# Four weight loads and splits moved within the projections of a two-branch attention kernel

## Chip, core and metric

The kernel runs on one NeuronCore of a Trainium2 chip. The metric is the device time of one execution in microseconds. Before the change it is 1011.23 us, the median of 3 runs (1010.02 to 1012.23).

The engines are named as in the profile: PE is TensorE's matrix multiply and PEld its weight load, DVE is VectorE, ACT is ScalarE, POOL is GpSimd. SP (SyncE) issues the DMAs, all of them here, in one queue.

## The reference

Input x has 2048 tokens of 448 features. Two attention layers with 16 heads of 28 features each run on the same x and are mixed by a gate for each token.

```python
x = A_x                                               # [1, 2048, 448]
g = _sigmoid((x * gate_w).sum(-1, keepdims=True))
# A: linear attention with the Hedgehog feature map
q, k, v = split_heads(x @ A_wqkv)
pq, pk = einsum("bhsd,hdf->bhsf", q, w_phi), einsum(..., k, w_phi)
phi_q = concat([softmax(pq), softmax(-pq)]); phi_k likewise
num = phi_q @ (phi_k^T v);  den = phi_q . sum_s(phi_k) + 1e-6
a = (num / den) @ A_wo
# B: softmax attention
q, k, v = split_heads(x @ B_wqkv)
b = (softmax(q k^T * 28 ** -0.5) v) @ B_wo
return g * a + (1 - g) * b
```

## The kernel before

**Numbers in two halves.** Matrices of the projections are kept as a high part in the type fp32r and a low part, which is the rest. A load from HBM therefore goes through a staging tile: a DMA brings the f32 values, ACT copies them to the high part, and DVE (in places POOL) subtracts the high part from the raw values and writes the low part. For x this gives XH and XL, for weights `w[:, 0]` and `w[:, 1]`. A projection of 512 tokens by 128 columns is 11 matmuls: four row blocks, each with high by high, high by low and (three of them) low by high.

**The order of work.** Each of the compute engines runs its instructions in the order in which the Python program gives them; an instruction waits on semaphores for what it reads and for the buffer that it overwrites. The order on SP's queue is chosen at build time by the scheduler of the language, from the dependences, so a load can move among the stores of other units when a dependence is added to it. SP issues in that order, and stands where an issue waits. Eight semaphores serve the DMAs in turn, so that an issue also waits until the DMA eight places before it has landed.

**The stage of the change.** The first 66 us compute queries and keys of branch B, transposed, in units: unit n is 128 of the 896 columns (m) for 512 tokens (t). `first_units` does units 0 to 3 (all of t = 0, m 0 to 3) while the weights' first 512 columns, wB[0], and x arrive. The loop `for n in range(4, NP)` does units 4 to 19:

- Units 4 to 7 take t = 1, units 8 to 11 t = 2, units 12 to 15 t = 3, all with wB[0]. Units 16 to 19 take m = 4 for the four t, with wB[1], the later 384 columns (wB1).
- `proj_qk(n, ev)` runs the 11 matmuls into a PSUM bank; `keep_qk` evacuates it. ACT (line 592) copies the bank to the high part of a tile `ev`, DVE (line 593) subtracts to its low part, and one DMA of 512 KB (line 594) stores both to the tensor `qkd` in DRAM. There are 4 buffers of `ev`.
- `splits(n + 1)` in round n splits what round n + 1 needs: x's tile t at the rounds 0, 4 and 8, and the two halves of wB1 in rounds 12 and 14.
- `fold(wkA_s, "k", g)` multiplies a quarter of the key weights of branch A (wtk, loaded by `load_fold`) by the folding matrix phi_s, which holds w_phi, so that the feature map's linear part costs no matmul of its own later. It is 4 calls of matmul (8 in the trace), an ACT copy (line 412) and a DVE subtraction (line 413).
- `split_part(wvA_s, "wvA", 450, i)` with `take_lows()` splits a half of the value weights of branch A (lines 143 and 144).
- `mx_unit()` in rounds 16 to 19 is a block of branch B's row maximum: four narrow matmuls into four banks (line 287), two ACT Relus (line 291) and two DVE additions with maximum (line 292). Later rounds have more of them.

The PSUM tiles of units and foldings share one ring of 3 banks (`ps_s`; units 4 to 6 use banks put aside in `later`), and the mx blocks have a ring of 4. After unit 19 the loop over tokens begins: `pk` (with wkA_s), `pva` (with wvA_s) and mx blocks.

**What holds a load back.** A DMA without a dependence may be issued as early as its place on the queue allows. The kernel delays some by letting POOL write a few elements into the destination first: the DMA overwrites them and so has to wait for the copy, which waits for what it reads.

```python
hold = raws[("x", 1)][0][:1, 0, :4]                        # in first_units
nc.gpsimd.tensor_copy(phi_s[:1, :, 0], hold)
...
nc.gpsimd.tensor_copy(wts[nm][:1, :, 0], phi_s[:1, :, 0])  # in load_fold, for "k"
```

So phi_s waits for x's tile 1, and wtk waits for phi_s. The load of wB1 (round 10) has no hold; its staging tile is one of three.

Of the kernel before, what the change touches and what calls it, by code (L numbers as in the profile page):

```python
# [36 lines left out]
def f32(ap):  # L37
    return ap.bitcast(F32)
# [3 lines left out]
def gated_mix_kernel(ctx, tc, xT, wqkB, wvB, wvA, wkAT, wqAT, phi, woA, woB,  # L42
# [7 lines left out]
    nc = tc.nc  # L50
# [12 lines left out]
    def ps_s(nm):  # L63
        return ps.tile([P, 512], F32, tag="s", name=nm, bufs=psn[0])

    def ps_pv(nm):
        return ps.tile([P, 512], F32, tag="pv", name=nm, bufs=1)

    def ps_mx(nm):
        return ps.tile([P, 512], F32, tag="mx", name=nm, bufs=psn[1])  # L70
# [22 lines left out]
    XH = front.tile([P, 4, S], F32R, name="XH")  # L93
# [6 lines left out]
    def weights(place, nm):  # L100
        if place == 1:
            return wp.tile([P, 2, 4, 512], F32R, tag="w1", name=nm)
        if place == 2:
            return front.tile([P, 2, 4, D], F32R, tag="w2", name=nm)
        return wp.tile([P, 2, 4, 450], F32R, tag="w3", name=nm)
# [21 lines left out]
            nc.tensor.matmul(dst[:, :n], l, r, start=i == 0, stop=i == len(todo) - 1,  # L127
                             skip_group_check=True)

    def stage(shape_b, n, src, nm):  # L130
        raw = stg.tile([P, 2, 512], F32, tag="stg", name=nm)
        nc.sync.dma_start(raw[:, :shape_b, :n], src)
        return raw[:, :shape_b, :n]

# [2 lines left out]
    def take_lows():  # L137
        while lows:
            lows.pop(0)()

    def split_weight(w, raw, bs, cs, low=nc.vector, high=nc.scalar.copy):

        high(w[:, 0, bs, cs], raw)
        lows.append(lambda: low.tensor_sub(w[:, 1, bs, cs], raw, f32(w[:, 0, bs, cs])))

    def load_part(src, n, nm, b, parts=2):
        return stage(parts, n, src[:, b:b + parts, :], f"{nm}_raw{b}")

    def weight_part(w, src, n, nm, b, parts=2, low=nc.vector):
        split_weight(w, load_part(src, n, nm, b, parts), slice(b, b + parts), slice(0, n), low)  # L150
# [14 lines left out]
    def take_acts():  # L165
        while acts:
            acts.pop(0)()
# [57 lines left out]
    def pair_query(gq, hp):  # L225
        g, qb = divmod(gq, NQ)
        mxs[("qp", gq, hp)] = mx_rows(mx_tile("qc", f"qp{gq}_{hp}", 3), range(4), q_d[g],
                                      (2 * hp, 2 * hp + 1) * 2, qb * 512)
# [130 lines left out]
    phi_s = bk.tile([112, NG, 112], F32, name="phi_s")  # L359
# [5 lines left out]
    def load_last(b):  # L365

        raw = bd.tile([P, H, 2, DH], F32, tag="feat", name=f"xraw3_{b}", bufs=4)
        raw = raw.rearrange("p h s f -> p (h s f)")[:, :512]
        nc.sync.dma_start(raw, xT[:, b, 1536:])
        return raw  # L370
# [25 lines left out]
    def load_fold(src, nm):  # L396
        wts[nm] = bk.tile([112, NG, 512], F32, tag="wt", name=f"wt{nm}", bufs=1)
        if nm == "k":
            nc.gpsimd.tensor_copy(wts[nm][:1, :, 0], phi_s[:1, :, 0])
        for k in range(NG):  # L400
            nc.sync.dma_start(wts[nm][:, k, :], src[:, k, :])

    def fold(dst, nm, g, b0=0, n=4):

        wt = wts[nm][:, g, :]
        pw = ps_s(f"pw{nm}{g}_{b0}")
        for b in range(n):
            nc.tensor.matmul(pw[:, b * 112:(b + 1) * 112], wt[:, (b0 + b) * P:(b0 + b + 1) * P],
                             phi_s[:, g, :], start=True, stop=True)
        pw3 = pw[:, :n * 112].rearrange("p (b f) -> p b f", f=112)  # L410
        bs, gs = slice(b0, b0 + n), slice(g * 112, (g + 1) * 112)
        nc.scalar.copy(dst[:, 0, bs, gs], pw3)
        nc.vector.tensor_sub(dst[:, 1, bs, gs], pw3, f32(dst[:, 0, bs, gs]))
# [166 lines left out]
    def proj_qk(n, ev):  # L580

        m, t = UNITS[n]
        tt = slice(t * 512, (t + 1) * 512)
        pq = later.pop(0) if later else ps_s(f"pqk{t}_{m}")
        w, c = wB[m // 4], m % 4 * P
        run(pq, [(w[:, i, b, c:c + P], x) for b, x, i in x3(tt)])
        keep_qk(m, t, pq, ev)

    def keep_qk(m, t, pq, ev):
        tt = slice(t * 512, (t + 1) * 512)  # L590
        e = ev.tile([P, 2, 512], F32R, tag="ev", name=f"ev{t}_{m}")
        nc.scalar.copy(e[:, 0, :], pq)  # L592
        nc.vector.tensor_sub(e[:, 1, :], pq, f32(e[:, 0, :]))  # L593
        nc.sync.dma_start(qk_d[m * P:(m + 1) * P, :, tt], f32(e))
# [7 lines left out]
    wkA_s = weights(2, "wkA_s")  # L602
    wvA_s = weights(3, "wvA_s")
    raws = {}

    def loads(key, *fns):
        raws[key] = [f() for f in fns]

    def x_loads(t):
        loads(("x", t), lambda: load_x(t, 0), lambda: load_x(t, 2))  # L610

    def part_loads(key, src, n, nm):
        loads(key, lambda: load_part(src, n, nm, 0), lambda: load_part(src, n, nm, 2))

    def split_part(w, key, n, i, low=nc.vector):
        split_weight(w, raws[key][i], slice(2 * i, 2 * i + 2), slice(0, n), low)

    def splits(n):

        if n % 4 == 1 and n < 12:  # L620
            split_x(n // 4 + 1, raws.pop(("x", n // 4 + 1)))
        if n in (13, 15):
            split_part(wB[1], "wB1", 384, (n - 13) // 2)
        take_lows()

    def first_units():

        raw = [stg.tile([P, 2, 512], F32, tag="stg", name=f"first_raw{b}") for b in range(3)]
        raw.append(f32(ev.tile([P, 2, 512], F32R, tag="ev", name="first_raw3")))
        for b in range(4):  # L630
            nc.sync.dma_start(raw[b][:, 0, :], wqkB[:, b, :512])
            nc.sync.dma_start(raw[b][:, 1, :], xT[:, b, :512])
        x_loads(1)
        pqs = [ps_s(f"pqk0_{m}") for m in range(3)] + [ps_pv("pqk0_3")]
        later.extend(ps_mx(f"pqk_{i}") for i in range(3))
        for _ in range(8):
            nc.tensor.matmul(pqs[3][:, :P], ident, ident, start=True, stop=True)
        for b in range(4):
            w, x = wB[0][:, :, b, :], XH[:, b, :512]
            nc.scalar.copy(w[:, 0, :], raw[b][:, 0, :])  # L640
            (nc.scalar.copy if b else nc.vector.tensor_copy)(x, raw[b][:, 1, :])
            nc.vector.tensor_sub(w[:, 1, :], raw[b][:, 0, :], f32(w[:, 0, :]))
            if b < 3:
                nc.vector.tensor_sub(XL[:, b, :512], raw[b][:, 1, :], f32(x))
                todo = [(0, x), (1, x), (0, XL[:, b, :512])]
            else:
                nc.vector.tensor_sub(x[64:], raw[b][64:, 1, :], f32(x[64:]))
                todo = [(0, x), (1, x)]
            if b < 3:
                order = [(i, m) for i in range(3) for m in range(4)]  # L650
            else:
                order = [(i, m) for m in range(4) for i in range(2)]
            for i, m in order:
                nc.tensor.matmul(pqs[m], w[:, todo[i][0], m * P:(m + 1) * P], todo[i][1],
                                 start=b == 0 and i == 0, stop=b == 3 and i == 1,
                                 skip_group_check=True)
        hold = raws[("x", 1)][0][:1, 0, :4]
        splits(1)
        nc.gpsimd.tensor_copy(phi_s[:1, :, 0], hold)
        for m in range(4):  # L660
            keep_qk(m, 0, pqs[m], ev)

# [3 lines left out]
    for n in range(4, NP):  # L666
        take_acts()
        if n == 4:
            x_loads(2)
            raws[("x", 3)] = [load_last(b) for b in range(4)]  # L670
        if n == 8:
            nc.sync.dma_start(phi_s, phi)
            load_fold(wkAT, "k")
        if n == 10:
            part_loads("wB1", wqkB[:, :, 512:896], 384, "wB1")
        splits(n + 1)
        if n == 14:
            part_loads("wvA", wvA, 450, "wvA")
            nc.sync.dma_start(sel_s, sel)
            nc.sync.dma_start(mask_s, mask)  # L680
            for v in vap:
                nc.gpsimd.memset(v[:, :, 28:32], 0.0)
                nc.gpsimd.memset(v[:, :, 28:29], 1.0)
        if 16 <= n < 20:
            mx_unit()
        proj_qk(n, ev)
        if n in (16, 18):
            split_part(wvA_s, "wvA", 450, (n - 16) // 2)
            take_lows()
        if n in (12, 14, 16, 18):  # L690
            fold(wkA_s, "k", {12: 0, 14: 1, 16: 2, 18: 3}[n])
        if n == 10:
            pair_query(0, 0)
            pair_load(0, 0)
        if n == 15:
            pair_load(0, 1)
            pair_query(0, 1)
        if n in (14, 19):
            take_subs()
# [447 lines left out]
    while s < NS + 16:  # L1147
        n = 2 if 0 < s <= first or LAST < s < NS - 1 else 1
# [22 lines left out]
        if 0 < steps[0] < NS:  # L1171
            heads = [(t, j) for t in steps for j in range(t in ahead, 4)]
            heads += [(s, 0)] * (s in ahead)
            b = cycle_banks(len(heads))
            for t in dict.fromkeys(t for t, _ in heads):
# [4 lines left out]
                b = b[len(js):]  # L1180
# [89 lines left out]
```

## Time and profile before

| | us |
|---|---|
| median of 3 runs | 1011.23 |
| lowest, highest | 1010.02, 1012.23 |
| the profiled execution's own time | 1012.12 |
| its span, first to last instruction | 1010.3 |
| its TensorE busy | 1003.4 |
| its ACT busy | 821.6 |
| its DVE busy | 647.0 |
| its POOL busy | 249.0 |

The mean granted clock of TensorE over the span is 0.998. A row of a timeline gives start and length in us, the engine (a q behind it means its sequencer, which waits or issues), the line, the operation, the tiles as out<-in, the partitions by elements and the count; in brackets stands how long the engine was idle before it and what released it. A row of the windows gives the stretch, its length, then the busy time and count of PE, PEld, DVE, ACT and POOL, then the granted clock, the busy share of the 16 DMA engines and GB/s. A row of the waits gives who waited for whom: total us, times, the longest.

### The profile page before, as it was taken

What the parts mean: (1) busy time and instruction counts of PE and PEld (TensorE: products, weight loads), DVE (VectorE), ACT (ScalarE), POOL (GpSimd) and SP (SyncE); (2) the same over time, 40 slices, a digit from 0 to 9 for tenths busy, and PEclk for the clock granted to TensorE, in tenths of its full rate; (3) what the DMA queues carried; (4) which work ended last, traced back from release to release, by engine and by line L of the source; (5) the groups of instructions that cost most, each with busy time, mean ns of one, the idle gap of its engine ahead of it and who ended that gap; (6) DMA issues with size and microseconds to landing.
All of it is one profiled execution on the core that took longest, in us unless ns stands there. A gap on an engine that the chain in (4) does not pass through costs nothing.

```text
span 1010.3 us, 18048 instructions
## 1 busy us (share of the span) xinstructions
PE 1003.4 (99%) x6344; PEld 566.2 (56%) x6344; DVE 647.0 (64%) x1336; ACT 821.6 (81%) x1614; POOL 249.0 (25%) x218
## 2 busy tenths in 40 slices
PE   9999999999999999999999999999999999999998
PEld 8777877877877754444444443333333333335665
DVE  5556767899765635454454468888888788885112
ACT  4455655587766699999999999999999999997662
POOL 1125544679634910310110110010120101100010
PEclk9999999999999999999999999999999999999999
DMA  9864010112233771223552234432232355610441
GB/s 307 304 221 127 32 52 31 43 50 83 81 105 95 164 155 38 63 59 83 107 110 49 68 80 90 104 77 65 70 79 66 67 122 144 148 38 30 137 146 55
DMA packets 64605, 99.64 MB, mean 99 GB/s; under 512 B 18166, under 2 KB 24934, under 8 KB 64514
## 3 DMA queue, kind: packets, MB, share of 16 engines
q1 hardware_dynamic: 64514, 98.49, 37.1%
q8 instruction: 50, 0.82, 0.4%
q14 instruction: 41, 0.34, 0.1%
HBM read 70.29 MB, written 27.78 MB: 97 GB/s over the span
## 4 chain that ended last, share of the span: by engine, by line
PE 93%; DVE 3%; DMA 3%; ACT 1%; issue 1%; SPq 0%; DVEq 0%; ACTq 0%
PE st L875 28%; PE pv L1015 24%; PE pm L324 8%; PE poa L109 4%; PE pk L127 4%; PE pva L127 4%; PE pqk L109 4%; PE pmd L287 3%; PE pob L109 3%; PE pq L109 2%; PE pvb L127 2%; PE pvb L109 2%; PE pn L553 1%; DMA xraw<-in_xT_dram 1%; PE pft L541 1%; DMA qkd<-ev 1%
## 5 line engine op out<-in xcount | busy, mean ns | idle before, releaser
L890 ACT ACTIVATE p<-st 128x512 f32<-128x512 f32 x1020 | 524.7, 635 | 26.4 <-PE st L875 26.4
L336 DVE TENSOR_REDUCE part<-pm 128x1 f32<-128x512 f32 x405 | 258.9, 686 | 179.1 <-PE pm L324 179.1
L875 PE MATMUL st<-qst,kst 128*128 128x512 f32 x1024 | 299.6, 422 | 0.0
L1015 PE MATMUL pv<-p,vb 128*32 128x512 f32 x2048 | 259.7, 601 | 0.0
L875 PEld LDWEIGHTS st<-qst,kst 128*128 128x128 f32 x1024 | 171.1, 187 | 101.4 <-ACT p L890 38.9
L440 POOL TENSOR_TENSOR oUb<-oUb,rsb 128x512 f32<-128x512 f32 x15 | 19.3, 1289 | 495.0 <-DMA rsb<-rdb 212.7
L292 DVE CUSTOM_DVE_ANT_0 rl<-pmb,rl 128x512 f32<-128x512 f32 x152 | 98.0, 682 | 46.6 <-ACT rl L291 46.6
L328 ACT ACTIVATE rl<-pm 128x512 f32<-128x512 f32 x180 | 111.3, 618 | 10.4 <-PE pm L324 9.2
L324 PEld LDWEIGHTS pm<-kc,qc 28*128 28x128 f32 x720 | 34.4, 181 | 150.9 <-ACT p L890 102.3
L291 ACT ACTIVATE rl<-pmd 128x512 f32<-128x512 f32 x152 | 83.1, 601 | 32.1 <-PE pmb L287 28.8
L1015 PEld LDWEIGHTS pv<-p,vb 128*32 128x32 f32 x2048 | 50.4, 108 | 96.0 <-issue 94.0
L333 DVE CUSTOM_DVE_ANT_0 rl<-pm,rl 128x512 f32<-128x512 f32 x135 | 92.0, 681 | 0.0
L324 PE MATMUL pm<-kc,qc 28*128 28x512 f32 x720 | 91.0, 495 | 0.0
L109 PE MATMUL pqk<-XH,wB 128*128 128x512 f32 x192 | 60.2, 402 | 0.5 <-DVE ev L593 0.5
L592 ACT CAST ev<-pqk 128x512 fp32r<-128x512 f32 x28 | 16.0, 589 | 39.9 <-PE pqk L109 27.2
L109 PE MATMUL poa<-woA_s,oTa 128*128 128x448 f32 x192 | 43.4, 375 | 0.0
L109 PEld LDWEIGHTS pqk<-XH,wB 128*128 128x128 f32 x192 | 35.8, 190 | 9.6 <-issue 1.5
L1026 DVE SCALAR_TENSOR_TENSOR acc<-pob,gate,acc 128x448 f32<-128x448 f32 x12 | 8.2, 684 | 50.8 <-PE pob L109 50.8
L287 PE MATMUL pmb<-kp,qp 28*128 28x512 f32 x152 | 39.1, 493 | 0.7 <-DVE part L292 0.4
L127 PE MATMUL pk<-wkA_s,XH 128*128 128x448 f32 x128 | 39.4, 382 | 0.0
L593 DVE TENSOR_TENSOR ev<-pqk,ev 128x512 fp32r<-128x512 f32 x28 | 18.9, 689 | 31.5 <-ACT ev L592 31.5
L287 PE MATMUL pmd<-kp,qp 28*128 28x512 f32 x152 | 38.5, 495 | 0.4 <-ACT rl L291 0.4
(159 smaller groups left out, 1212.1 us busy)
## 6 DMA issues: line engine op xcount, KB each, us to landing
qkd<-ev SPq DMA_DIRECT2D x28, 512.0 KB
qst<-qkd SPq DMA_DIRECT2D x64, 224.0 KB
kst<-qkd SPq DMA_DIRECT2D x64, 224.0 KB
od<-oTb SPq DMA_DIRECT2D x48, 112.0 KB
rsa<-rda SPq DMA_DIRECT2D x8, 512.0 KB
rsb<-rdb SPq DMA_DIRECT2D x15, 256.0 KB
gad<-ga SPq DMA_DIRECT2D x16, 224.0 KB
acc<-gad SPq DMA_DIRECT2D x4, 896.0 KB
```

The costliest lines, as they stand in the source:

```text
L109: nc.tensor.matmul(dst, l, r, start=i == 0, stop=i == len(todo) - 1)
L127: nc.tensor.matmul(dst[:, :n], l, r, start=i == 0, stop=i == len(todo) - 1, skip_group_check=True)
L287: nc.tensor.matmul(pm[j], qc[js, qt * P:(qt + 1) * P], kc[js, :], start=True, stop=True, tile_position=(32 * i, 0))
L291: nc.scalar.activation(rl, pm[i], AF.Relu)
L292: nc.vector.tensor_tensor_reduce(rl, pm[2 + i], rl, 1.0, LOWEST, ALU.add, ALU.max, part[:, col + i:col + i + 1])
L324: nc.tensor.matmul(pm[j], mxs[("qc", gq)][js, qt * P:(qt + 1) * P], mxs[("kc", g, kb)][js, :], start=True, stop=True, tile_position=(32 * ...
L328: nc.scalar.activation(rl, pm[kb], AF.Relu if kb < 3 else AF.Copy)
L333: nc.vector.tensor_tensor_reduce(r, pm[j], r, 1.0, LOWEST, ALU.add, ALU.max, part[:, col + j:col + j + 1])
L336: nc.vector.tensor_reduce(part[:, col + j:col + j + 1], pm[j], AX.X, ALU.max)
L875: nc.tensor.matmul(st, kst_of[(g, kt // 4)][:, j, (kt % 4) * P:(kt % 4 + 1) * P], qst_of[gq][:, j, :], start=True, stop=True)
L890: nc.scalar.activation(p, sts[j], AF.Exp, scale=SCALE)
L1015: nc.tensor.matmul(pv[32 * j:32 * j + 32, :], vb[kt // 8][:, kt % 8, 4 * g + j, :], pt[j], start=kt == 0, stop=kt == NT - 1, tile_position ...
```

## The change

Four things. The copy that holds phi_s now reads the first elements of XH of x's tile 2 and stands in round 8, right before the load. The load of wB1's first half gets a hold of its own, from XH of x's tile 3; `stage`, `load_part` and `part_loads` pass it on. wvA is split in rounds 17 and 19, not 16 and 18. The foldings are done in rounds 13, 14, 15 and 16, not 12, 14, 16 and 18.

```diff
-    def stage(shape_b, n, src, nm):
+    def stage(shape_b, n, src, nm, after=None):
         raw = stg.tile([P, 2, 512], F32, tag="stg", name=nm)
+        if after is not None:
+            nc.gpsimd.tensor_copy(raw[:1, 0, :4], after)
         nc.sync.dma_start(raw[:, :shape_b, :n], src)
         return raw[:, :shape_b, :n]
...
-    def part_loads(key, src, n, nm):
-        loads(key, lambda: load_part(src, n, nm, 0), lambda: load_part(src, n, nm, 2))
+    def part_loads(key, src, n, nm, after=None):
+        loads(key, lambda: load_part(src, n, nm, 0, 2, after), lambda: load_part(src, n, nm, 2))
...
-        hold = raws[("x", 1)][0][:1, 0, :4]
         splits(1)
-        nc.gpsimd.tensor_copy(phi_s[:1, :, 0], hold)
...
         if n == 8:
+            nc.gpsimd.tensor_copy(phi_s[:1, :, 0], f32(XH[:1, 0, 1024:1028]))
             nc.sync.dma_start(phi_s, phi)
             load_fold(wkAT, "k")
         if n == 10:
-            part_loads("wB1", wqkB[:, :, 512:896], 384, "wB1")
+            part_loads("wB1", wqkB[:, :, 512:896], 384, "wB1", f32(XH[:1, 0, 1536:1540]))
         splits(n + 1)
...
         proj_qk(n, ev)
-        if n in (16, 18):
-            split_part(wvA_s, "wvA", 450, (n - 16) // 2)
+        if n in (17, 19):
+            split_part(wvA_s, "wvA", 450, (n - 17) // 2)
             take_lows()
-        if n in (12, 14, 16, 18):
-            fold(wkA_s, "k", {12: 0, 14: 1, 16: 2, 18: 3}[n])
+        if n in (13, 14, 15, 16):
+            fold(wkA_s, "k", {13: 0, 14: 1, 15: 2, 16: 3}[n])
```

On SP's queue as built, this moves loads: before, phi and wB1's first half stand behind the last part of x and ahead of the first store of a unit, wtk's four quarters about the store of unit 7, and wB1's second half behind that of unit 9. After, phi stands behind the store of unit 6, wtk behind that of unit 7, and both halves of wB1 behind that of unit 9. From the store of unit 11 on the order is the same until late in the kernel.

More of the change, by code (lines that the diff above doesn't have):

```diff
@@ L144, in split_weight, with load_part @@
         lows.append(lambda: low.tensor_sub(w[:, 1, bs, cs], raw, f32(w[:, 0, bs, cs])))
-    def load_part(src, n, nm, b, parts=2):
-        return stage(parts, n, src[:, b:b + parts, :], f"{nm}_raw{b}")
+    def load_part(src, n, nm, b, parts=2, after=None):
+        return stage(parts, n, src[:, b:b + parts, :], f"{nm}_raw{b}", after)
     def weight_part(w, src, n, nm, b, parts=2, low=nc.vector):
```

## The prediction

> **What bounds the kernel now.** I read the page first, then who makes TensorE wait in the first 110 us (every line of the diff runs there), then that stretch's timelines and windows.
>
> ```profile
> span 1010.3 us, 18048 instructions
> ...
> PE 1003.4 (99%) x6344; PEld 566.2 (56%) x6344; DVE 647.0 (64%) x1336; ACT 821.6 (81%) x1614; POOL 249.0 (25%) x218
> ...
> PE 93%; DVE 3%; DMA 3%; ACT 1%; issue 1%; SPq 0%; DVEq 0%; ACTq 0%
> ```
>
> TensorE is busy from end to end and is 93% of the chain that ended last. A stall saved or added early therefore moves the end by its own length; an edit that only moves ACT, DVE or DMA work is worth what it does to TensorE. The view of TensorE's waits up to 110 us has four that the diff can touch:
>
> ```profile
> PE pqk L109 <- DVE ev L593: 0.5, 1, 0.5
> PE pmd L287 <- ACT rl L291: 0.4, 1, 0.4
> PE pmb L287 <- DVE part L292: 0.4, 1, 0.4
> PE pmb L287 <- ACT rl L291: 0.2, 1, 0.2
> ```
>
> These are only gaps between matmul records. The real loss shows in TensorE's timeline (start, length, line, count), where two full matmuls in a row advance the stream by 0.45 us:
>
> ```profile
> 31.85 0.61 PE L109 MATMUL pqk<-XH,wB 128*128 128x512 f32 x2
> 33.01 0.73 PE L109 MATMUL pqk<-XH,wB 128*128 128x512 f32 x2 [0.54 <-DVE ev L593]
> ...
> 38.13 1.04 PE L408 MATMUL pwk<-phi_s,wtk 112*128 112x112 f32 x8
> 38.94 0.70 PE L109 MATMUL pqk<-XH,wB 128*128 128x512 f32 x2
> ...
> 54.26 0.63 PE L109 MATMUL pqk<-XH,wB 128*128 128x512 f32 x2
> 55.26 0.99 PE L287 MATMUL pmd<-kp,qp 28*128 28x512 f32 x2 [0.37 <-ACT rl L291]
> ...
> 57.72 0.73 PE L109 MATMUL pqk<-XH,wB 128*128 128x512 f32 x2
> ...
> 61.48 1.52 PE L408 MATMUL pwk<-phi_s,wtk 112*128 112x112 f32 x8
> 62.92 0.50 PE L287 MATMUL pmd<-kp,qp 28*128 28x512 f32 x2
> ...
> 66.13 0.50 PE L287 MATMUL pmd<-kp,qp 28*128 28x512 f32 x2
> ```
>
> Stall one, unit 11: due 31.85 + 0.45 = 32.30, begins 33.01, 0.7 us lost. From 33.01 to 38.13 are two units: 2.55 us each. Stall two, the row-maximum (mx) block between units 16 and 17: unit 16 ends its stream at 54.71, the block needs 0.44 (62.92 to unit 19's start at 63.36), unit 17 begins at 57.72 instead of 55.15: 2.6 us lost. Then unit 17 takes 3.76 us (57.72 to 61.48) in place of 2.55, and the folding behind it 1.44 (to 62.92) in place of 0.81 (38.13 to 38.94). Windows say why (last three columns: granted clock, DMA share, GB/s):
>
> ```profile
> 52.23:55.64 3.41, 3.04 (x12) 2.00 (x12) 1.33 (x2) 2.31 (x5) 0.00 (x0) 1.00 1.05 387
> 55.64:59.06 3.42, 2.87 (x10) 1.67 (x10) 3.34 (x10) 1.72 (x4) 0.72 (x1) 1.00 0.55 159
> 59.06:62.47 3.41, 3.41 (x12) 2.83 (x11) 0.10 (x1) 0.71 (x2) 1.83 (x2) 0.50 0.90 324
> 30.00:33.40 3.40, 2.86 (x13) 2.04 (x13) 3.18 (x4) 2.23 (x5) 2.26 (x9) 1.00 0.95 272
> ```
>
> After stall two TensorE has half its clock for 3.4 us: 1.21 + 0.63 = 1.8 us. Stall one (last row) cost no clock. So 0.7 + 2.6 + 1.8 = 5.1 us hang on what the diff touches.
>
> **The cause of each.** ACT's timeline:
>
> ```profile
> 24.26 0.59 ACT L592 CAST ev<-pqk 128x512 fp32r<-128x512 f32 x1 [5.09 <-DMA qkd<-ev]
> ...
> 28.00 0.59 ACT L592 CAST ev<-pqk 128x512 fp32r<-128x512 f32 x1 [0.68 <-DMA qkd<-ev]
> ...
> 36.32 0.84 ACT L143 CAST wB<-wB_raw 128x768 fp32r<-128x768 f32 x1
> ...
> 53.33 0.95 ACT L143 CAST wvA_s<-wvA_raw 128x900 fp32r<-128x900 f32 x1 [1.89 <-DMA wvA_raw<-in_wvA_dram]
> ...
> 66.28 0.59 ACT L592 CAST ev<-pqk 128x512 fp32r<-128x512 f32 x1 [1.67 <-issue]
> ```
>
> Four evacuations (units 4 to 7, 24.26 to 28.00, so 1.25 us apart) wait for the stores of units 0 to 3 to land, since ev has four buffers. That lateness reaches unit 11 through its PSUM bank. Stall two is the row at 53.33: ACT stands before the first half of wvA, and behind it on ACT are a folding's evacuation and the mx block's Relus.
>
> **The change, part by part.** The DMA queue first (SP's timeline, then its waits between 40.8 and 42.6 us, then POOL's timeline, then two rows of the chain up to 85 us with issue time and time to landing):
>
> ```profile
> 14.64 0.43 SPq L672 DMA_DIRECT2D phi_s<-in_phi_dram  x1
> 15.18 0.39 SPq L132 DMA_DIRECT2D wB_raw<-in_wqkB_dram  x1
> ...
> 34.21 1.06 SPq L132 DMA_DIRECT2D wB_raw<-in_wqkB_dram  x1
> ...
> 40.92 1.62 SPq L176 DMA_DIRECT2D kp<-qkd  x2
> ```
>
> ```profile
> SPq L176 <- DMA wB_raw<-in_wqkB_dram: 0.2, 1, 0.2
> ```
>
> ```profile
> 21.01 0.18 POOL L399 COPY wtk<-phi_s 1x4 f32<-1x4 f32 x1
> ```
>
> ```profile
> 1.19 2.98 DMA first_raw<-in_xT_dram
> ...
> 14.08 5.97 DMA xraw<-in_xT_dram
> ```
>
> ```profile
> 22.00:24.00 2.00, 2.00 (x11) 1.65 (x10) 0.00 (x0) 0.00 (x0) 0.00 (x0) 1.00 1.05 404
> 38.00:40.00 2.00, 2.00 (x15) 1.79 (x14) 0.76 (x3) 1.02 (x2) 0.00 (x0) 1.00 0.96 362
> ```
>
> (a) *Holding phi and wB1.* Today phi (196 KB) and the first half of wB1 (384 KB) stand between x's last part, landed at 14.08 + 5.97 = 20.05, and the stores of units 0 to 3. In the built order both now come later: phi behind the store of unit 6, wB1 behind that of unit 9. 594 KB (580 KiB) at 404 GB/s is 1.5 us, by which the stores land earlier and ACT's four evacuations come earlier. Unit 11's bank needs 0.7: stall one goes. Value −0.7; bounds −0.7 and 0. The two copies on POOL that hold the loads cost what L399's does, 0.18 us each, one more than today, on an engine with nothing late behind it but the low part of x's last tile, which unit 12 needs only near 36: nothing.
>
> (b) *What that makes late: wB1's first half.* Today, issued at 15.18, it is there long before ACT splits it at 36.32. In the new order everything that landed before the second half does today is also ahead of the two halves, which now go back to back. Today the second half lands at about 40.9 (the issue at 40.92 waited 0.2 us for it). In a queue that never empties the first half is one half-load before that: 393 KB at 362 GB/s is 1.1, so 39.8. But the queue empties once: wtk is held by POOL until phi has landed. Unit 6's store would be issued near 26.7, phi near 27.2; stores 4 to 6 land 1.25 apart from about 27.6 (issue 24.0 plus the store's own length on a queue just run dry), phi at 30.7, wtk is issued at 31.0, and on an empty queue 2.98 us pass to landing (row at 1.19; it is 256 KB, the same order of size): 34.0, where an unbroken queue would have it near 33.2. That adds 0.8: 40.6. Bounds 39.0 (the queue some 0.8 faster without the early loads mixed in) and 41.6 (the gap twice as long).
>
> ACT's order there is: evacuate unit 11, split wB1's first half, evacuate units 12, 13. So unit 12's bank, which unit 14 needs, comes free at landing + 0.87 (ACT) + 0.87 (DVE's low part) + 0.7 (DVE's evacuation) + 0.05, about landing + 2.5:
>
> ```profile
> 37.19 0.96 DVE L144 TENSOR_TENSOR wB<-wB_raw,wB 128x768 fp32r<-128x768 f32 x1
> 39.38 0.69 DVE L593 TENSOR_TENSOR ev<-pqk,ev 128x512 fp32r<-128x512 f32 x1 [1.24 <-ACT ev L592]
> ```
>
> TensorE wants that bank at 32.30 + 3 × 2.55 + 0.81 (the first folding, now behind unit 13) = 40.8. Bank free at 43.1: a new stall of 2.3 us before unit 14; bounds 0.7 and 3.3.
>
> (c) *wvA split a unit later.* ACT reaches the first half after unit 17, near 57, when it has landed even if 3 us later than today. Stall two goes: −2.6, and with it −1.8 of clock; bounds −4.4 and −2.6 (if the clock halves all the same, d). But the split now stands directly before an mx block's Relus and maxima, with no folding on TensorE to cover it:
>
> ```profile
> 63.22 1.10 DVE L144 TENSOR_TENSOR wvA_s<-wvA_raw,wvA_s 128x900 fp32r<-128x900 f32 x1 [0.15 <-ACT wvA_s L143]
> ...
> 65.37 0.69 DVE L292 CUSTOM_DVE_ANT_0 rl<-pmb,rl 128x512 f32<-128x512 f32 x1
> ```
>
> From an mx start T: evacuation at T + 0.15 (66.28 after 66.13), wvA's high part T + 0.6 to 1.6, low part to T + 2.7, two maxima of 0.6 each to T + 3.9. The next block is due at T + 3.1 (0.44 and a unit with its restart) after unit 17, T + 3.3 after unit 19, and uses the same four banks: 0.8 and 0.6 us of stall, +1.4 together; bounds 0.5 and 1.8.
>
> (d) *Clock.* A 2.3 us stall with no matmul in it is about as long as stall two, which had narrow ones in it and was followed by half clock; stall one, 0.7, was not. By these rows it halves the clock in some executions: +1.7 or 0. The runs of before, 1010.02 to 1012.23, are themselves as far apart as one such spell. The Trainium skill (TensorE: Matmul & The Clock Gate, "What's actually happening") says that half rate returns after at least one idle window of some 3.4 us on a free-running clock. The trace has the 3.4 us as the spell's length, but its window 55.64:59.06 was 2.87 us busy, so a whole idle window wasn't needed here; by the page's rule the new stall would cost no clock, and the time would be 1010.7.
>
> (e) *Foldings after units 13 to 16.* The same eight matmuls each (0.81 us), so the stream is as long. Two evacuations leave the places in which a wvA split stood: their gain is in (c). The first folding moves from 38.13 to near 40: wtk's first quarter, at 34.0 above, is ready. Nothing; −0.2 to +0.3.
>
> **Sum**, against the profiled execution's own 1012.12 (span 1010.3 and 1.8 around it): −0.7 − 2.6 − 1.8 + 2.3 + 1.4 = −1.4, so 1010.7 with a full clock, 1012.4 with one new spell at half clock. A median of several runs lies between: 1011.5. The profiled execution stands 0.9 above the median shown, 1011.23, since it holds a spell that, as said, not all runs need have.
>
> **The rivals.** *Faster, by loads in time:* the first half of wB1 lands at 39.0 or before; the new stall is 0.7 at most and keeps its clock: 1012.12 − 5.1 + 0.7 + 1.1 = 1008.8. For it: stores land 1.5 us earlier. Against: the DMA share is 0.96 at 38 to 40 and wtk waits for phi. *Slower, by the held load:* a longer gap in the queue, first half at 41.6, stall 3.3, always long enough for half clock: 1012.12 − 5.1 + 3.3 + 1.8 + 1.7 = 1013.8. It decides from a landing near 41.4. For it: two holds in series (x, phi, wtk) before wB1. *The split doesn't help:* wvA lands so late (later than 57) that ACT stands there again: −0.7 + 2.3 + about 1 of stall on top of the old, 1014.7. Against: it lands at 53.3, and the queue's order behind wB1 is unchanged.
>
> **How the numbers follow.** About 0.2%, 2 us, is what can be told from no change: 1009.2 to 1013.3. Forecast (1010.7 to 1012.4) 0.52, faster rival 0.2, slower 0.23, split without help 0.05. The forecast's own spread passes either bound a little: faster 0.24, same 0.47, slower 0.29. Range 1008.6 to 1014.2, from the faster rival to a little past the slower; the forecast's own 1010.0 to 1013.2.
>
> **What would show it.** Right: no wait of TensorE near 33; a wait for ev's DVE step before unit 14, with ACT idle before wB's split for DMA wB_raw; no ACT wait for wvA_raw; short waits of the mx blocks behind units 18 and 19; half clock, if at all, near 42 to 46. Wrong: ACT's first wB split without a wait, or TensorE idle at a folding for wtk.

## The result, and the profile after

| | before | after |
|---|---|---|
| median of 20 runs each, us | 1010.33 | 1013.36 |
| lowest, highest | 1009.64, 1012.88 | 1011.37, 1016.11 |
| ratio, 95% interval | | 1.0026 [1.0017, 1.0034] |
| the profiled execution's own time | 1012.12 | 1015.72 |
| its span | 1010.3 | 1013.9 |

The change makes the kernel 0.26% slower. The median lies in the predicted range, but above the forecast's own 1010.0 to 1013.2: it is 1.9 us above the predicted value and next to the rival "slower, by the held load" (1013.8). The profiled execution of the changed kernel is the third slowest of its 20, so what follows of it shows where the time goes and not how much a usual execution loses.

From the page of the profile of the changed kernel:

```profile
span 1013.9 us, 18054 instructions
...
PE 1004.2 (99%) x6344; PEld 567.1 (56%) x6344; DVE 646.6 (64%) x1336; ACT 821.3 (81%) x1614; POOL 248.8 (25%) x219
```

TensorE's busy time is 0.8 us longer and the span 3.6, so most of the loss is idle TensorE. Of the four waits of before, the view of TensorE's waits up to 110 us has none left, and one new one that is longer than all four together:

```profile
PE pqk L109 <- DVE ev L595: 4.1, 1, 4.1
```

(The numbers of the lines from 132 to 654 are 2 higher than before: 595 is 593 of before, 289 is 287.) TensorE's timeline around that wait, and at the two mx blocks that come after a split of wvA:

```profile
40.08 1.04 PE L410 MATMUL pwk<-phi_s,wtk 112*128 112x112 f32 x8
45.25 1.22 PE L109 MATMUL pqk<-XH,wB 128*128 128x512 f32 x2 [4.13 <-DVE ev L595]
...
49.94 1.04 PE L410 MATMUL pwk<-phi_s,wtk 112*128 112x112 f32 x8
...
64.78 0.50 PE L289 MATMUL pmd<-kp,qp 28*128 28x512 f32 x2
...
66.30 0.73 PE L109 MATMUL pqk<-XH,wB 128*128 128x512 f32 x2
...
72.33 0.50 PE L289 MATMUL pmd<-kp,qp 28*128 28x512 f32 x2
...
73.47 0.48 PE L127 MATMUL pva<-wvA_s,XL 128*128 128x450 f32 x1
```

The folding at 40.08 is the one behind unit 13. Unit 14 is due 0.81 later, at 40.89, and begins at 45.25: 4.36 us lost. It lasts to 49.94, 4.69 in place of 2.55, so 2.1 more. The mx block behind unit 18 takes 1.52 where 0.44 is needed: 1.1. The one in the first value tile takes 1.14: 0.7.

ACT's and DVE's timelines name the cause of the first:

```profile
35.29 0.59 ACT L594 CAST ev<-pqk 128x512 fp32r<-128x512 f32 x1 [1.91 <-PE pqk L109]
42.77 0.83 ACT L145 CAST wB<-wB_raw 128x768 fp32r<-128x768 f32 x1 [6.89 <-DMA wB_raw<-in_wqkB_dram]
43.51 1.06 ACT L594 CAST ev<-pqk 128x512 fp32r<-128x512 f32 x2
```

```profile
43.63 0.96 DVE L146 TENSOR_TENSOR wB<-wB_raw,wB 128x768 fp32r<-128x768 f32 x1 [7.03 <-ACT wB L145]
44.51 1.28 DVE L595 TENSOR_TENSOR ev<-pqk,ev 128x512 fp32r<-128x512 f32 x2
```

ACT stands 6.89 us before the split of wB1's first half, until its load lands near 42.7. Only then do the evacuations of units 12 and 13 follow on ACT and, behind the low part of the weights, on DVE, whose first one ends near 45.2: that frees the bank which unit 14 takes at 45.25.

The windows of the 3.4 us in which the new wait begins and of the two behind it (stretch, length, busy time and count of PE, PEld, DVE, ACT, POOL, then clock, DMA share, GB/s):

```profile
39.47:42.88 3.41, 1.65 (x12) 1.35 (x10) 0.00 (x0) 0.11 (x1) 0.00 (x0) 1.00 1.00 339
42.88:46.30 3.42, 1.05 (x3) 0.87 (x4) 2.67 (x5) 2.86 (x5) 0.00 (x0) 0.50 0.58 200
46.30:49.71 3.41, 3.41 (x10) 2.67 (x9) 0.89 (x2) 0.00 (x0) 2.60 (x2) 0.50 0.88 320
```

The clock is halved for 6.83 us, two stretches of 3.41, of which TensorE works through the second and a part of the first.

**The balance.** A useful yardstick is the time on TensorE from the first matmul of unit 4 to the first of `pk`, which holds every line of the diff that can stall it. Before it is 51.7 us (14.85 to 66.56); the shortest that any kernel below had is 46.8, and there no unit waits. After it is 54.4 (15.14 to 69.50). The 7.6 above 46.8 are 4.4 + 2.1 + 1.1. Together with the 0.7 in the first value tile and a first unit that came 0.3 later, the changed kernel's profile is 2.7 + 0.7 + 0.3 = 3.7 us longer than that of before; the spans differ by 3.6.

### The profile page after: what moved, and what is told of

The parts are those of the page before. It is cut to its first block, busy times and chain, and to the rows that moved or that the text cites. A ratio compares the mean times of both kernels' runs of the same rounds, so it can differ in the third digit from the quotient of the medians.

```text
span 1013.9 us, 18054 instructions
## 1 busy us (share of the span) xinstructions
PE 1004.2 (99%) x6344; PEld 567.1 (56%) x6344; DVE 646.6 (64%) x1336; ACT 821.3 (81%) x1614; POOL 248.8 (25%) x219
## 4 chain that ended last, share of the span: by engine, by line
PE 93%; DVE 4%; SPq 1%; issue 1%; POOL 1%; ACT 1%; DMA 0%; DVEq 0%; POOLq 0%; ACTq 0%
PE st L876 28%; PE pv L1016 24%; PE pm L326 8%; PE pqk L109 5%; PE poa L109 4%; PE pk L127 4%; PE pva L127 3%; PE pmd L289 3%; PE pob L109 3%; PE pvb L127 2%; PE pvb L109 2%; PE pq L109 1%; PE pn L555 1%; PE pqk L656 1%; PE pft L543 1%; DVE fsumq L479 1%
## 5 line engine op out<-in xcount | busy, mean ns | idle before, releaser
L109 PEld LDWEIGHTS poa<-woA_s,oTa 128*128 128x128 f32 x192 | 34.9, 188 | 6.2 <-issue 3.2
```

The lines of the kernel that those rows point to most:

```text
L109: nc.tensor.matmul(dst, l, r, start=i == 0, stop=i == len(todo) - 1)
```

## The experiments

All were run in 5 rounds beside the kernel before, 11 or 12 executions of each. The medians of before in the three groups were 1010.41 (e1 to e4), 1010.08 (e5 to e8) and 1010.15 (e9 to e11). Each version has one profile, and it isn't always of a usual execution: those of e6 and e11 are the fastest of their runs, those of e3 and e9 the second fastest, that of e1 the slowest.

| | version | median us | ratio to before [95%] | unit 4 to pk, us |
|---|---|---|---|---|
| e1 | after, wB1 not held | 1009.31 | 0.9982 [0.9973, 0.9992] | 47.6 |
| e2 | after, wB1's halves split two rounds and one round later | 1009.95 | 0.9989 [0.9979, 1.0000] | 48.7 |
| e3 | before, wB1 held | 1011.64 | 1.0001 [0.9990, 1.0012] | 49.6 |
| e4 | before, wvA later, foldings in a row | 1010.24 | 0.9992 [0.9982, 1.0001] | 48.1 |
| e5 | after, again | 1011.90 | 1.0012 [1.0000, 1.0024] | 50.1 |
| e6 | after, phi held as before | 1011.61 | 1.0006 [0.9995, 1.0016] | 48.9 |
| e7 | before, wvA later | 1009.00 | 0.9982 [0.9974, 0.9990] | 46.8 |
| e8 | before, wvA later, phi's hold of after | 1009.12 | 0.9984 [0.9975, 0.9992] | 46.8 |
| e9 | e7, second low part behind the mx block | 1008.60 | 0.9980 [0.9971, 0.9989] | 46.8 |
| e10 | before, foldings in a row | 1010.23 | 0.9996 [0.9987, 1.0005] | 49.7 |
| e11 | before, phi's hold of after | 1009.73 | 0.9994 [0.9982, 1.0005] | 49.0 |

### The hold of wB1: e1, e2, e3, e5

e1 takes the one hold out of the changed kernel:

```diff
-            part_loads("wB1", wqkB[:, :, 512:896], 384, "wB1", f32(XH[:1, 0, 1536:1540]))
+            part_loads("wB1", wqkB[:, :, 512:896], 384, "wB1")
```

> The changed kernel without the hold on wB1; phi held, wvA and foldings as changed. Theory (the held load): TensorE's 4.1 us wait before unit 14 and the half clock behind it are gone, ACT's first wB split has no wait for a DMA; stall one (33) and stall two (55) stay away, the mx blocks behind units 17 and 19 still wait 1.2 and 0.7; against before 0.9975 to 0.9990. Rival 1 (the splits and foldings at their new places cost it): still slower than before, 1.001 or more. Rival 2 (phi's hold, which lets the queue run dry, costs it): wtk is as late, TensorE waits at the foldings or before unit 14, 1.001 or more.

ACT's split then follows its evacuation at once, and unit 14 (the third row, TensorE) starts when the folding behind unit 13 (the second) lets it, 0.81 later:

```profile
36.80 0.84 ACT L145 CAST wB<-wB_raw 128x768 fp32r<-128x768 f32 x1
```

```profile
41.10 1.04 PE L410 MATMUL pwk<-phi_s,wtk 112*128 112x112 f32 x8
41.91 0.70 PE L109 MATMUL pqk<-XH,wB 128*128 128x512 f32 x2
```

The view of TensorE's waits has no row left but the one from the program's first instructions. With the other three edits in place the kernel is faster than before; the hold of wB1 turns 0.9982 into 1.0026, or 1.0012 in the second group of runs of the changed kernel (e5). The intervals do not touch.

e2 keeps every hold and splits wB1 later (`splits(n + 1)` runs in round n, so in rounds 14 and 15, not 12 and 14), when ACT need not stand for it:

```diff
-        if n in (13, 15):
-            split_part(wB[1], "wB1", 384, (n - 13) // 2)
+        if n in (15, 16):
+            split_part(wB[1], "wB1", 384, n - 15)
```

> The changed kernel with all its holds; only ACT and DVE split wB1's halves in rounds 14 and 15 instead of 12 and 14, so behind the evacuations of units 12 and 13. Theory: the first half lands as late as in the changed kernel (42 to 43) and costs nothing, as nothing that TensorE needs stands behind it; no wait before unit 14; against before 0.9975 to 0.9990, level with the run without the hold. Rival 2 (the queue is late for all, stores and kp with it): TensorE waits elsewhere between 40 and 50, 1.001 or more. Rival 1: 1.001 or more.

```profile
41.59 0.54 ACT L414 CAST wkA_s<-pwk 128x448 fp32r<-128x448 f32 x1 [0.29 <-PE pwk L410]
42.02 0.84 ACT L145 CAST wB<-wB_raw 128x768 fp32r<-128x768 f32 x1
```

```profile
40.51 1.04 PE L410 MATMUL pwk<-phi_s,wtk 112*128 112x112 f32 x8
41.32 0.70 PE L109 MATMUL pqk<-XH,wB 128*128 128x512 f32 x2
```

The evacuations and the first folding (41.59) now go ahead of the split on ACT, there is no wait for the load, and unit 14 starts 0.81 behind the folding. The load is held as in the changed kernel. So it isn't the late load as such that costs time, but that ACT stands before it with evacuations queued behind.

e3 adds the hold of wB1 to the kernel before (`stage`, `load_part` and `part_loads` pass it on as in the change), and nothing else:

```diff
-            part_loads("wB1", wqkB[:, :, 512:896], 384, "wB1")
+            part_loads("wB1", wqkB[:, :, 512:896], 384, "wB1", f32(XH[:1, 0, 1536:1540]))
```

> The kernel before with the hold on wB1 alone. Theory: ACT stands before wB1's first half from about 36, which lands at 40 to 42; TensorE waits 2 to 4 us before unit 14, perhaps with half clock behind it; part of that is taken off stall two, which is shorter or gone as TensorE comes there later; against before 1.000 to 1.004. Rival 2: without phi's hold the half lands by 38.5, no wait, 0.999 to 1.001.

```profile
39.15 0.83 ACT L145 CAST wB<-wB_raw 128x768 fp32r<-128x768 f32 x1 [3.20 <-DMA wB_raw<-in_wqkB_dram]
```

```profile
41.63 0.73 PE L109 MATMUL pqk<-XH,wB 128*128 128x512 f32 x2 [0.40 <-DVE ev L595]
```

The wait on ACT is there (3.20), but the load comes at 39.1 and unit 14 loses half a microsecond, where 2 to 4 us were put down. Alone the hold can't be told from no change by the ratio (1.0001), though its median is 1.2 us above that of before. Whether it needs the other hold to become dear isn't shown.

e5 is the changed kernel once more:

> The changed kernel once more, for a second profile on the chip of the other runs here. Theory: the same places as in the first profile, with a first half of wB1 that lands between 40 and 43 and a wait before unit 14 of that landing plus 2.5 us less 40.9 plus what the first units began later; half clock behind it if it is over 2 us; against before 1.001 to 1.0035. If the first profile's 4.1 us was a single bad execution, the wait is under 1 us and the ratio under 1.001.

```profile
40.20 0.83 ACT L145 CAST wB<-wB_raw 128x768 fp32r<-128x768 f32 x1 [3.58 <-DMA wB_raw<-in_wqkB_dram]
```

```profile
40.82 1.04 PE L410 MATMUL pwk<-phi_s,wtk 112*128 112x112 f32 x8
42.68 0.73 PE L109 MATMUL pqk<-XH,wB 128*128 128x512 f32 x2 [0.82 <-DVE ev L595]
```

The same program has the load at 40.2 here and at 42.8 in its first profile, and loses 1.05 us before unit 14 in place of 4.36, with the clock at full speed. The DMA queue says where the time went. The first fence is the first profile's windows, the second those of e5, the third one of before:

```profile
22.00:24.00 2.00, 2.00 (x11) 1.65 (x10) 0.21 (x1) 0.59 (x1) 0.00 (x0) 1.00 0.72 271
24.00:26.00 2.00, 2.00 (x10) 1.68 (x9) 1.17 (x2) 1.04 (x2) 0.00 (x0) 1.00 0.25 95
...
32.00:34.00 2.00, 2.00 (x11) 1.65 (x10) 0.58 (x1) 0.59 (x1) 1.89 (x8) 1.00 0.53 151
34.00:36.00 2.00, 2.00 (x11) 1.65 (x9) 0.20 (x2) 0.59 (x1) 0.43 (x5) 1.00 0.87 244
```

```profile
24.00:26.00 2.00, 2.00 (x10) 1.65 (x10) 0.69 (x1) 0.47 (x1) 0.00 (x0) 1.00 1.03 392
...
30.00:32.00 2.00, 2.00 (x11) 1.65 (x10) 0.50 (x2) 0.59 (x1) 1.77 (x10) 1.00 0.76 228
32.00:34.00 2.00, 2.00 (x10) 1.67 (x9) 0.36 (x1) 0.46 (x1) 0.04 (x1) 1.00 0.91 288
```

```profile
26.00:28.00 2.00, 2.00 (x11) 1.65 (x9) 1.34 (x2) 0.67 (x2) 0.00 (x0) 1.00 0.68 255
```

In the first profile the queue runs dry twice. Between 22 and 26 its shares of 0.72 and 0.25 are 2.1 us lost: ACT evacuates unit 4 only at 23.17, when the store of unit 0 has landed, so there is no next store to issue. Before has this gap too, but it is shorter (0.86 between 24 and 26 and 0.68 behind it, 0.9 us). e11, which holds phi alone, has 1.3 (a share of 0.36 between 24 and 26). In e5, the same program as the first profile, ACT has the buffer at 20.86 and there is hardly a gap. So the holds alone don't make it, and why the store of unit 0 landed 2.3 us later in the first profile than in e5 isn't shown. Between 32 and 36, after phi and before wtk's data, the first profile loses 1.2 more; in e5 this second gap is 0.7.

### The hold of phi: e6, e8, e11

e6 is the changed kernel with phi held as before, on the raw tile 1 of x:

```diff
+        hold = raws[("x", 1)][0][:1, 0, :4]
         splits(1)
+        nc.gpsimd.tensor_copy(phi_s[:1, :, 0], hold)
...
-            nc.gpsimd.tensor_copy(phi_s[:1, :, 0], f32(XH[:1, 0, 1024:1028]))
```

> The changed kernel with phi held as before the change; the hold on wB1, wvA and foldings as changed. Theory: wtk no longer waits for a late phi, the queue doesn't run dry, and wB1's first half lands about 1 us sooner (39 to 40.5); the wait before unit 14 is 0.5 to 1.5 us less than in the changed kernel but there; against before 0.9985 to 1.001. Rival 2 (phi's hold is the cause): no wait before unit 14, 0.9975 to 0.9990. Rival 1 (wB1's hold alone, phi's is harmless): as the changed kernel, 1.001 or more.

```profile
38.68 0.84 ACT L145 CAST wB<-wB_raw 128x768 fp32r<-128x768 f32 x1 [2.93 <-DMA wB_raw<-in_wqkB_dram]
```

POOL's timeline of the changed kernel (first profile) and that of e6, in each the copies that hold wtk and wB1:

```profile
31.95 0.18 POOL L401 COPY wtk<-phi_s 1x4 f32<-1x4 f32 x1 [10.16 <-DMA phi_s<-in_phi_dram]
...
33.32 0.18 POOL L133 COPY wB_raw<-XH 1x4 f32<-1x4 f32 x1
```

```profile
21.44 0.18 POOL L401 COPY wtk<-phi_s 1x4 f32<-1x4 f32 x1
29.31 0.66 POOL L133 COPY wB_raw<-XH 1x4 f32<-1x4 f32 x1
```

With phi early, wtk's copy is done at 21.4 and doesn't wait for phi at 32, and wB1's copy, which stands behind it in POOL's program, comes at 29.3 in place of 33.3. wB1 lands at 38.7, 1.5 us before e5's and 4.1 before the first profile's, and TensorE loses 0.4 us before unit 14 (39.94 + 0.81 to 41.16). So in these profiles the two holds in series make wB1 later than one does. That this costs time isn't shown: e6's 1.0006 can't be told from e5's 1.0012, nor from before. Among the runs with a mean clock of 0.999 or more the medians are 1011.2 in e6 and 1011.1 in e3, which hold wB1 alone, 1011.7 in e5 and 1010.0 in before. By these the hold of wB1 costs about 1 us already without the hold of phi.

e8 takes the hold of wB1 out of the changed kernel, as e1 does, and puts the foldings back; what is left is the later split and the new hold of phi:

```diff
-        if n in (13, 14, 15, 16):
-            fold(wkA_s, "k", {13: 0, 14: 1, 15: 2, 16: 3}[n])
+        if n in (12, 14, 16, 18):
+            fold(wkA_s, "k", {12: 0, 14: 1, 16: 2, 18: 3}[n])
```

> The changed kernel without the hold on wB1 and with the foldings at 12, 14, 16 and 18: phi held and wvA later are left of the change. Theory: as the run without the hold on wB1, less the 1.1 us wait behind unit 18, if wtk (landed near 37) is in time for the folding behind unit 12: against before 0.9965 to 0.9985. Rival: the folding at 38 waits for wtk and gives it back, 0.9985 or more.

e11 is the kernel before with the new hold of phi alone:

```diff
-        hold = raws[("x", 1)][0][:1, 0, :4]
         splits(1)
-        nc.gpsimd.tensor_copy(phi_s[:1, :, 0], hold)
...
+            nc.gpsimd.tensor_copy(phi_s[:1, :, 0], f32(XH[:1, 0, 1024:1028]))
             nc.sync.dma_start(phi_s, phi)
```

> The kernel before with phi's hold on x's tile 2 and nothing else; wB1 comes early as before. The prediction's term for the holds (the stores of units 0 to 3 land earlier, stall one before unit 11 goes): 0.3 to 0.7 us faster, ratio 0.9993 to 0.9997. Rival (phi's place on the queue changes nothing that TensorE waits for, and stall one comes and goes with the start of the full clock in each execution): ratio 0.9997 to 1.0005. If wtk comes too late for the first folding in round 12, TensorE waits there and it is slower: 1.001 or more.

e8's 0.9984 is e7's 0.9982: phi's hold adds nothing that can be told to the later split, and the folding behind unit 12 doesn't wait for wtk in e8 or e11. In e11 the last of ACT's four evacuations that wait for stores comes at 26.96 in place of 28.00, as the prediction's part (a) wanted it:

```profile
26.96 0.59 ACT L592 CAST ev<-pqk 128x512 fp32r<-128x512 f32 x1 [0.65 <-DMA qkd<-ev]
```

and unit 11 doesn't wait. But 0.9994 [0.9982, 1.0005] can't be told from nothing, nor can the 0.7 us of stall one: e7 has the old hold, and no stall before unit 11 either. Its first units came 1.3 us later (unit 4 at 16.13 in place of 14.85), and the banks were free in time.

### The split of wvA and the foldings: e4, e7, e10, e9

e7 is the kernel before with the split of wvA moved and nothing else:

```diff
-        if n in (16, 18):
-            split_part(wvA_s, "wvA", 450, (n - 16) // 2)
+        if n in (17, 19):
+            split_part(wvA_s, "wvA", 450, (n - 17) // 2)
```

> The kernel before with wvA split in rounds 17 and 19 alone, foldings at 12, 14, 16 and 18. Theory: stall two is gone, and the mx block behind unit 18 no longer waits, since the folding in round 18 stands between; only the one in the first value tile waits 0.6 to 0.8; so 0.8 to 1.2 us better than with the foldings in a row: against before 0.9970 to 0.9988. Rival (the foldings in a row are what lets the split go later): stall two or a wait at a folding comes back, 0.9995 or more.

TensorE's timeline behind unit 18 and in the first value tile:

```profile
58.35 1.04 PE L408 MATMUL pwk<-phi_s,wtk 112*128 112x112 f32 x8
59.32 0.50 PE L287 MATMUL pmd<-kp,qp 28*128 28x512 f32 x2
...
65.79 0.50 PE L287 MATMUL pmd<-kp,qp 28*128 28x512 f32 x2
65.89 1.10 PE L287 MATMUL pmb<-kp,qp 28*128 28x512 f32 x2
66.92 0.48 PE L127 MATMUL pva<-wvA_s,XL 128*128 128x450 f32 x1
```

The gain is here: 1.08 us of median, and in none of its 12 runs was the mean clock below 0.999. The folding behind unit 18 (58.35) stays in its old place and gives ACT and DVE the 0.8 us that the mx block needs.

e4 has e7's edit and the foldings in a row, without holds; e10 has the foldings in a row alone:

```diff
-        if n in (12, 14, 16, 18):
-            fold(wkA_s, "k", {12: 0, 14: 1, 16: 2, 18: 3}[n])
+        if n in (13, 14, 15, 16):
+            fold(wkA_s, "k", {13: 0, 14: 1, 15: 2, 16: 3}[n])
```

> The kernel before with wvA split in rounds 17 and 19 and the foldings in rounds 13 to 16, no new hold. Theory: stall two and its half clock are gone, waits of about 1.2 and 0.7 behind units 17 and 19 come; stall one (0.7) stays; against before 0.9980 to 0.9992. Rival 1: 1.001 or more.

> The kernel before with the foldings in rounds 13 to 16 and nothing else. wvA's split stays in rounds 16 and 18, before the mx blocks. Theory (a folding on TensorE covers the mx block behind a split, and taking it away costs about 1 us): slower than before by 0.5 to 1.5 us, ratio 1.0005 to 1.0015, with stall two still there and a loss at the mx block behind unit 18. Rival (the prediction's own term: the foldings' places are worth nothing by themselves): ratio 0.9998 to 1.0003.

Without the folding, the mx block behind unit 18 begins at 59.06 in e4 and unit 19 at 60.73: 1.67 where 0.44 would do, 1.2 us lost, and that is the whole difference of the yardstick between e4 and e7 (48.1 and 46.8). e4's 0.9992 can't be told from before: with the foldings in a row the later split has hardly a gain left. By the medians, each beside its own group's before, it is 0.9 us, but the two intervals overlap. In e10 the foldings alone cost nothing (0.9996): the theory put down for that run falls, its rival holds. There the split still stands before the block between units 17 and 18, which waits in the old way:

```profile
57.54 0.49 PE L287 MATMUL pmb<-kp,qp 28*128 28x512 f32 x1 [0.46 <-ACT rl L291]
```

So the foldings' places have a price only together with the later split, which moves the need for cover to the block that they no longer stand before.

e9 goes on from e7. It leaves the second half's low part until the mx block at the start of the first value tile has been issued:

```diff
             split_part(wvA_s, "wvA", 450, (n - 17) // 2)
-            take_lows()
+            if n == 17:
+                take_lows()
...
             mx_unit()
+            if t == 0:
+                take_lows()
```

> The kernel before with wvA split in rounds 17 and 19, and the low part of its second half issued behind the mx block that opens the first value tile, ahead of the tile's pk. Theory (the 0.7 us lost at the second mx block of the first value tile is DVE's low part standing before the block's maxima): that loss goes, ratio about 0.7 us below that of the version with the later split alone (0.9982), so 0.9975, and TensorE's mx blocks in the first value tile come without a gap. Rival (the low part only changes places, and the maxima of the next block or the value matmuls wait for it): ratio 0.998 to 0.9985 and the gap shows one block later.

DVE's timeline of e7 and of e9, then TensorE's of e9:

```profile
64.13 1.10 DVE L144 TENSOR_TENSOR wvA_s<-wvA_raw,wvA_s 128x900 fp32r<-128x900 f32 x1 [0.15 <-ACT wvA_s L143]
65.14 0.68 DVE L292 CUSTOM_DVE_ANT_0 rl<-pmb,rl 128x512 f32<-128x512 f32 x1
```

```profile
63.72 0.69 DVE L292 CUSTOM_DVE_ANT_0 rl<-pmb,rl 128x512 f32<-128x512 f32 x1 [0.65 <-ACT rl L291]
...
64.95 1.09 DVE L144 TENSOR_TENSOR wvA_s<-wvA_raw,wvA_s 128x900 fp32r<-128x900 f32 x1
```

```profile
64.88 0.50 PE L287 MATMUL pmd<-kp,qp 28*128 28x512 f32 x2
...
65.51 0.48 PE L127 MATMUL pva<-wvA_s,XL 128*128 128x450 f32 x1
```

The mx block in the value tile takes 0.63 in place of 1.13, and the next ones don't wait, as the theory says and not the rival, though the ratio is the rival's. The median is the lowest of all, 1008.60, 0.15% below before, with a ratio that beats both kernels; that it also beats e7 (0.9980 against 0.9982) isn't shown.

## Why the prediction was right or wrong

**What bounds the kernel: right.** The 3.6 us of the changed kernel's profile are TensorE's, from the places named.

**A unit's number: wrong by one, without effect on the sum.** The prediction put stall two "between units 16 and 17". The foldings of before at 38.13 and 61.48 follow units 12 and 18, so the unit from 57.72 to 61.48 is unit 18, and stall two lies between 17 and 18.

**(a) The holds free the queue for the stores: right in mechanism, worth less.** ACT evacuates unit 7 at 27.1 to 28.3 in the five profiles with both loads early (before, e4, e7, e9, e10) and at 25.7 to 27.0 in the eight that hold one or both, on the mean 1.4 us earlier, where 1.5 was worked out. Unit 11 waits in none of these eight. But e8 against e7 and e11 against before show no gain that can be told from none. Stall one comes in two of the five profiles with both loads early: 0.7 us where unit 4 began at 14.85 (before), a wait of 0.2 at 15.41 (e10), none at 15.22 (e9), 15.87 (e4) and 16.13 (e7). So the prediction took a loss of some executions for one of all.

**(b) wB1's first half late, and unit 14 waits for it: right in place and cause, the landing too early.** ACT stands before the split, then evacuates units 12 and 13, and unit 14 begins 2.5 us after the landing, as worked out: 42.8 to 45.25, and 40.2 to 42.68 in e5. The step that failed is the landing, "the queue empties once", put at 40.6 with bounds of 39.0 and 41.6. The first profile has 42.8, outside the bounds. There the queue ran dry twice. The second gap, the one that was forecast, lost 1.2 us in place of 0.8. The first, near 24, lost 1.2 more than the one that before has there (2.1 and 0.9), and the prediction has no term for that. Together this is 1.6 of the 2.2 us by which the landing was late; the rest isn't traced. In e5 the first gap didn't occur, and the landing was 0.4 from the forecast. The stall was 4.36 and 1.05 us in the two profiles, where the term had 2.3. Neither need be a usual one: at full clock the median is 1012.0 with the hold of wB1 and 1009.3 without it (e1), so the hold costs 2.7 us there, near the term.

**(c) wvA's split later: the gain right, the price of the next mx block right only for a part.** Stall two is gone in every kernel with the later split. But the yardstick of before is 51.7 in its one profile, while e3, e10 and e11, which keep the split in its old place, have 49.0 to 49.7 at full clock with a stall two of some 1.5 us: the profile shown was one of the third of the runs of before in which the clock halves. The sum had a gain of 3.0 us for this term (4.4 less the 1.4 of the mx blocks). Measured by medians it is 0.2 with the foldings in a row, as the changed kernel has them (e4, not told from nothing), and 1.1 with the foldings in their old places (e7). The block behind unit 18 cost 1.1 in the first profile and 2.2 in e5 (60.16 to 62.80, less 0.44), where 0.8 was forecast with a bound of 1.8 for both blocks. The one in the first value tile cost 0.7, as the 0.6 said.

**(d) The clock: right.** Half clock came behind the stall of 4.1 us without a matmul, and not behind one of 0.8 (e5). The runs fall apart by it. Of the 32 runs of the changed kernel, 13 have a mean clock of 0.998 or 0.996 and a median of 1013.9; the other 19 have 1012.0. Of the 99 runs of before beside the experiments, 32 have 0.997 or 0.998 and a median of 1012.5; the other 67 have 1010.0. (One spell of 3.41 us at half clock takes 1.7 off 1010, which is 0.998.) So the median hides two kinds of runs, and among those at full clock the change is 2.0 us slower. The Trainium skill (TensorE: Matmul & The Clock Gate, "What's actually happening") asks for a whole idle window of about 3.4 us. The stretch 39.47:42.88, which went before the half clock, was busy for 1.65 us, so here too less than a whole idle one was enough; that the clock changes in steps of 3.41 us agrees.

**(e) Foldings in a row cost nothing: right alone, wrong in company.** e10 shows nothing; but with the split moved the missing folding uncovers the mx block behind unit 18, 0.8 to 1.2 us by the profiles of e1 and e4 against those of e7 and e8. The prediction saw that no folding covers the block and booked it to the split.

**The rivals.** "Slower, by the held load" is what happened, with nearly its time; its mechanism, a long gap in the queue behind two holds in series, is there, but the larger gap was another. Its landing of 41.4 or later was met in the first profile and not in e5. "Faster, by loads in time" is what e1 shows: with wB1 in time the kernel takes 1009.3, where 1008.8 was worked out (with 1.1 for the mx blocks, where the sum has 1.4). "The split doesn't help" fell with e7.

**The sum.** The forecast had 1012.4 with one spell at half clock. Against it the first profile, 1015.7, has 2.1 more in the stall (4.36 for 2.3), 0.4 more in the clock, and 0.4 in the mx blocks; the remaining 0.4 is the later first unit and rounding. For the median the account is another. Without the new stall the forecast is 1008.4 (1012.12 − 5.1 + 1.4), and e1 takes 1009.3. The execution that the sum starts from had the earliest unit 4 of all 13 profiles (14.85, on the mean 15.5), which by this count is the larger part of the 0.9. With the stall the forecast is 1010.7 at full clock, and the changed kernel takes 1012.0 there: the stall adds the other 0.4. Most executions of before also have less to save than that one: their median was 1010.33 in 20 runs and not the 1011.23 of 3, so the change costs 3.0 us where the prediction had 0.3. That the result lies within the range is owed to the rival, for whose sake the range was wide; the forecast's own spread missed it by 0.2.

## What to carry to other kernels

Before a load is held back, look at what is queued behind the instruction that consumes it: on an engine that runs in order a late weight costs nothing where its split stands behind the evacuations (e2), and whole microseconds where it stands ahead of them. A chain of holds that starts later (x, phi, wtk) can leave the DMA queue empty where the early one didn't, so count the empty stretches of the queue and not only its bytes. When work on ACT and DVE is moved by a unit, check which matmuls now stand beside it as cover, and compare several profiles before a stall in one of them is priced.

## What the runs showed of the hardware

**A DVE subtraction that waits for POOL.** In e5 the low part of wvA takes 2.23 us, where it takes 1.10 in the other profile of the same kernel. POOL's and DVE's timelines of e5, then TensorE's:

```profile
57.49 2.65 POOL L223 TENSOR_TENSOR kp<-kp,kt 28x512 fp32r<-28x512 f32 x2 [10.36 <-DMA kt<-qkd]
```

```profile
58.87 2.23 DVE L146 TENSOR_TENSOR wvA_s<-wvA_raw,wvA_s 128x900 fp32r<-128x900 f32 x1
```

```profile
61.76 1.10 PE L289 MATMUL pmb<-kp,qp 28*128 28x512 f32 x2 [1.11 <-DVE part L294]
```

POOL's two subtractions end at 60.14. From there to DVE's end at 61.10 are 0.96 us, about what the DVE subtraction needs alone: it seems to have begun only when POOL was done, and the mx block's maxima and TensorE behind it were 1.1 us late. In e7 DVE came first (56.86), took its 1.10, and POOL's pair took 3.01. The Trainium skill (SBUF — State Buffer, "SBUF: two separate sides") says that the two share a port pair, which an instruction of POOL, or one of DVE with two inputs in SBUF as here, holds for its whole length while the other waits; the row agrees. The same subtraction takes 1.84 us in e2, 1.67 in e6 and 1.55 in e4, each beside POOL's pair. The mx block behind unit 18 loses 1.2 to 2.2 us in these three and e5, and 0.8 and 1.1 in e1 and the first profile, where the subtraction takes 1.10. So a part of what e4 loses there, some 0.5 us, is this and not the missing folding. It may be one cause of the spread between the runs: which of the two comes first seems to depend on when kt lands.

**The start differs from run to run.** Unit 4 begins between 14.85 and 16.17 us in the profiles, whatever the kernel, since TensorE comes to full clock at another time in each. By the clock records of the traces that is 4.4 us after the start of the span in the profile of before and 7.6 in e1's, and the first eight matmuls of 128x512 take 2.08 and 3.36 us there. The later the full clock, the later unit 4 begins, in all 13 profiles but for e3 and e9, which are 0.04 us apart. That alone makes 1.3 us, more than most of the edits here, and has a part in whether stall one occurs.
